# Gated linear attention and SwiGLU on one core: one ordered load queue, part of the transposes by DMA, and new positions for the key, query and output work

## The chip, the cores and the metric

The kernel runs on one core of a Trainium2 chip. A core has a matrix engine (TensorE, PE in the profile, its weight loads apart as PEld), VectorE (DVE), ScalarE (ACT), GpSimd (POOL), and SyncE (SP), which here only issues transfers. All engines run their own queue of instructions in order and wait for one another through semaphores. The metric is device microseconds of one execution; lower is better.

## The reference

For 2048 tokens `x` of width 640, a sigmoid gate mixes two branches: linear attention with a learned softmax feature map (32 heads of 20), and a SwiGLU feed-forward layer of width 1728.

```python
g   = sigmoid((x * gate_w).sum(-1))
q, k, v = split_heads(x @ wqkv)                    # 32 heads of 20
pq, pk  = q @ w_phi[h], k @ w_phi[h]
phi_q = concat(softmax(pq), softmax(-pq));  phi_k likewise
kv  = phi_k^T v ;  z = sum over tokens of phi_k    # per head
o   = (phi_q kv) / (phi_q z + 1e-6)
a   = o @ wo
b   = (silu(x @ w_gate) * (x @ w_up)) @ w_down
out = g * a + (1 - g) * b
```

## The kernel before

Tokens go in 16 tiles of 128; four tiles are a block of 512. All weights stay in SBUF. The whole program is written as work items, each with a position (a number): `put(pos, fn, ...)` collects them, they are sorted, and emitted in that order, so every engine sees its instructions in the order of the positions. `defer(n, fn)` holds a part of an item back until n items (its own among them) are emitted.

The items are:

- `xpose`: transposes a tile of x on PE (5 matmuls with an identity, out of the buffer `xs`), copied by DVE to `xT`. `wxpose`: the same for a 128-row chunk of wk or wq, to `wT`.
- `premult`: multiplies the transposed chunk with the block-diagonal `wbd` of w_phi (built by POOL), so that `wqk` holds wk or wq already times w_phi; its copy out of PSUM is ACT's.
- `vtile` (in short v): x times wv, and in column 641 x times the gate weight (`wvg`), copied by ACT to `v1r` and `svec`.
- `ktile` (k): x times wk-phi, two exponentials on ACT into `ekr`, sums (`ksum`) and reciprocals (`krec`) on DVE, the scaling product on POOL. `kvtile` (kv): 11 matmuls that add phi_k^T v to PSUM banks 6 and 7, over all 16 tiles.
- `kv_finish`, `z_broadcast`: kv and z out of PSUM, z spread over all partitions (`zb`).
- `fitem` (f): one 128-column chunk of gate and up, 10 matmuls of 512 columns, tanh and copy on ACT, one op on DVE (`hT<-hT,ps`, which reads PSUM), one product on POOL. 14 chunks a block; the last is half as long (`wt`).
- `qtile` (q): x times wq-phi, exponentials on ACT into `eq`, then a chain `vec` on DVE (sum `qz`, product `ez` with zb, sum `qw`, five small ops up to `qc`), a product on POOL (`ph`), and a transposing DMA from SP (`phiT`).
- `oitem` (o): 11 matmuls, phi_q times kv, for a block. `ditem` (d): 38 matmuls of 320 columns, the down projection and wo for a tile; ACT scales, SP stores.

PSUM has 8 banks. `next_pair` hands out pairs of banks in a ring, 3 pairs while kv collects in banks 6 and 7, 4 after `widen`. An item must wait until the item that had its pair is read out.

Waits come from a tracker: each operand is an interval of bytes in a partition, and an instruction waits for the writers and readers of all intervals that overlap its own. An operand with strides counts as one interval from its first to its last byte. `wvg[:, :, 0:640]` and its gate column overlap by this rule.

Loads: SP loads tiles of x into six buffers `xs`; tile t+6 is loaded when tile t is transposed. ACT loads wv, wk, wq. POOL loads the gate weight as a column (2-byte elements) and w_phi. The feed-forward weights come at position -0.5 (`load_ffn_weights`, from SP), before the first k.

The first items have positions -10 to -4; k of tile t is at t, kv at t+2.7, v at t-1.2 (from tile 4); f of block 0 from 15.7 on, 0.65 apart; the blocks behind it, from S1 = 24.8 on, have 17.0 each.

Of the kernel before, what the change touches and what calls it, by code (L numbers as in the profile page):

```python
# [14 lines left out]
NCH = 11  # L15
FP = 120 * NCH
# [9 lines left out]
class _Tracker:  # L26
# [32 lines left out]
    def key_of(self, ap):  # L59
        if isinstance(ap, tuple):  # L60
            key = ap
        else:
            space, base = self.base[ap.tensor.name]
            row = 1
            for s in ap.tensor.shape[1:]:
                row *= s
            size = mybir.dt.size(ap.dtype)
            lo = hi = ap.offset % row
            for step, n in list(ap.ap)[1:]:
                if n <= 1:  # L70
                    continue
                if step >= 0:
                    hi += step * (n - 1)
                else:
                    lo += step * (n - 1)
            lo, hi = base + lo * size, base + (hi + 1) * size
# [4 lines left out]
        if key not in self.keyset:  # L81
            self.keyset.add(key)
            self.keys[key[0]].append(key)
            self.lastw[key] = None
            self.readers[key] = {}
        return key
# [18 lines left out]
    def run(self, eng, fn, reads=(), writes=(), dma=False):  # L105
        rkeys = [self.key_of(a) for a in reads]
        wkeys = [self.key_of(a) for a in writes]
# [49 lines left out]
def _build(nc, A_x, A_wqkv, A_w_phi, A_wo, B_x, B_w_gate, B_w_up, B_w_down, gate_w, out):  # L157
# [33 lines left out]
    v1r = sb("v1r", [P, 4, 33 * 21], BF16)  # L191
# [31 lines left out]
    wqn = at("wqn", [P, 5, D], BF16, 14080)  # L223
# [3 lines left out]
    bmask = at("bmask", [P, 5, 8], BF16, 28736)  # L227

# [31 lines left out]
    def transposes(pairs):  # L260
        def fn():
            last = None
            for o, i in pairs:
                last = pe.transpose(o, i, ident[:, :])  # L264
            return last
        return run("pe", fn, [i for _, i in pairs] + [ident[:, :]], [o for o, _ in pairs])
# [53 lines left out]
    def load_x(t):  # L320
        dma("sp", xs[:, t % 6, :], x2[t * P:(t + 1) * P, :])

    load_x(0)
    load_x(1)
    wv_src = A_wqkv[:, 2 * D:3 * D].rearrange("(c p) j -> p c j", p=P)
# [3 lines left out]
    with nc.allow_non_contiguous_dma(reason="gate_w as a column of each chunk"):  # L329
        dma("pool", wvg[:, :, D:D + 1],  # L330
            bass.AP(gate_w.tensor, gate_w.offset, [[1, P], [P, 5], [1, 1]]))
    dma("pool", wph[:, :, :], A_w_phi.rearrange("h e f -> (h e) f").rearrange("(c p) f -> p c f", p=P))
    for t in range(2, 6):
        load_x(t)
    dma("act", wkn[:, :, :], A_wqkv[:, D:2 * D].rearrange("(c p) j -> p c j", p=P))
    dma("act", wqn[:, :, :], A_wqkv[:, 0:D].rearrange("(c p) j -> p c j", p=P))
# [14 lines left out]
    memset("dve", v1r[:, :, :], 0.0)  # L351
# [49 lines left out]
    def xpose(t0, n):  # L401
        pr = next_pair()
        for j in range(n):
            t = t0 + j
            b = 2 * pr + j
            o = bankbf(b, 640)
            transposes([(o[:, c * P:(c + 1) * P], xs[:, t % 6, c * P:(c + 1) * P]) for c in range(5)])
            copy("dve", xT[:, t, :, :].rearrange("p c k -> p (c k)"), o)
            if t + 6 < NT:
                load_x(t + 6)  # L410

    def vtile(t):
        pr = next_pair()
        mm(group(bank(2 * pr, 0, 320), [(xT[:, t, c, :], wvg[:, c, 0:320]) for c in range(5)])
           + group(bank(2 * pr + 1, 0, 321), [(xT[:, t, c, :], wvg[:, c, 320:641]) for c in range(5)]))
        i = halves(pr).rearrange("p b (h d) -> p b h d", d=DH)
        o = v1v[:, t % 4, 0:H, 0:DH].rearrange("p (b h) d -> p b h d", b=2)
        copy("act", o, i)
        copy("act", svec[:, t:t + 1], bank(2 * pr + 1, 320, 321))
# [7 lines left out]
    def tok_proj(t, which):  # L427
        pr = next_pair()
        mm(group(bank(2 * pr, 0, 320), [(xT[:, t, c, :], wqk[:, which, c, 0:320]) for c in range(5)])
           + group(bank(2 * pr + 1, 0, 320), [(xT[:, t, c, :], wqk[:, which, c, 320:640]) for c in range(5)]))  # L430
        return pr

    def ktile(t):
        pr = tok_proj(t, 1)
# [11 lines left out]
    def kvtile(t):  # L446
        b = t % 4
        pairs = []
        for j in range(NCH):
            bk, jj = (KV0, j) if j < 8 else (KV0 + 1, j - 8)  # L450
            o = bank(bk, 63 * jj, 63 * jj + 63, 0, 120)
            pairs.append((o, ekr[:, b, 120 * j:120 * j + 120], v1r[:, b, 63 * j:63 * j + 63],
# [3 lines left out]
    def wxpose(src, m):  # L456
        pr = next_pair()
        o = bankbf(2 * pr, 640)
        transposes([(o[:, c * P:(c + 1) * P], src[:, m, c * P:(c + 1) * P]) for c in range(5)])
# [7 lines left out]
    def premult(which, m):  # L467
        pr = next_pair()
        pairs = []
        for i, (hb, c, c0, c1, off) in enumerate(BANDS):  # L470
            o = bank(2 * pr + hb, c0 - 320 * hb, c1 - 320 * hb)
            pairs.append((o, wT[:, m, c, :], wbd[:, c, off:off + c1 - c0], i in (0, 3), i in (2, 5), True))
        mm(pairs)
        copy("act", wqk[:, which, m, :].rearrange("p (b c) -> p b c", b=2), halves(pr))
# [39 lines left out]
    def qtile(t):  # L514
# [6 lines left out]
        def vec():  # L521
# [201 lines left out]
```

## Time and profile before

| what | value |
|---|---|
| runs | 325.64, 326.25, 327.75 us; median 326.25 us |
| profiled execution, its own time | 327.81 us |
| its span | 326.1 us |
| mean granted PE clock | 0.99 |
| busy share of the span: PE, DVE, ACT, POOL | 92%, 54%, 46%, 47% |
| HBM read and written | 12.56 MB, 2.62 MB |

The span is the time from the first to the last instruction in the profile. A busy PE is the union of matmul records, which overlap their neighbours; what PE needs for an item is read from the start of one item to the start of the next where nothing waits.

### The profile page before, as it was taken

To read this page: it belongs to the slowest core of one execution; us is meant where nothing else is said; L and a number is where in the kernel's file an instruction comes from. 1 tells how busy PE (TensorE), PEld (TensorE's weight loads), DVE (VectorE), ACT (ScalarE), POOL (GpSimd) and SP (SyncE) were. 2 spreads that over 40 slices of the span, in tenths; PEclk is the share of its full clock that TensorE was granted. 3 is DMA by queue.
4 is the path that set the end of the run, shared out by engine and by line. 5 is a ranking of instruction groups with operands and counts; after the bars stand their busy time and mean duration, and the time that the engine had idled before them with its cause. 6 is when DMAs were issued, how large, how long until landed. Compare 5 with 4: busy or idle time off the path is not lost.

```text
span 326.1 us, 4990 instructions
## 1 busy us (share of the span) xinstructions
PE 301.0 (92%) x2041; PEld 182.5 (56%) x2041; DVE 177.5 (54%) x266; ACT 151.4 (46%) x254; POOL 153.4 (47%) x117
## 2 busy tenths in 40 slices
PE   1697899999898986979999999999999999999995
PEld 1364677777444543526555556565554656555773
DVE  6332766675964999892961126697203659721000
ACT  1045466666435654664532643625346363526111
POOL 3500845666784477874372422455624245563000
PEclk9997999999999999979999999999999999999999
DMA  7868962000000033222023000222200022220101
GB/s 261 244 201 278 356 130 77 2 1 2 0 2 1 0 68 66 45 46 64 0 54 78 2 20 0 66 45 64 66 20 0 2 64 46 64 64 2 40 22 40
DMA packets 36077, 21.26 MB, mean 65 GB/s; under 512 B 23816, under 2 KB 36056, under 8 KB 36056
## 3 DMA queue, kind: packets, MB, share of 16 engines
q1 hardware_dynamic: 34024, 18.47, 21.9%
q10 hardware_dynamic: 1968, 2.46, 2.3%
q8 instruction: 16, 0.26, 0.3%
q0 software_dynamic: 64, 0.03, 0.1%
q14 instruction: 5, 0.04, 0.0%
HBM read 12.56 MB, written 2.62 MB: 47 GB/s over the span
## 4 chain that ended last, share of the span: by engine, by line
PE 80%; DVE 9%; ACT 4%; DMA 4%; POOL 1%; issue 1%; POOLq 0%
PE ps L252 79%; DMA wvg<-in_gate_w_dram 2%; DVE qw L291 2%; DVE qz L291 2%; DVE ez L280 2%; DMA wvg<-in_A_wqkv_dram 2%; PE ps L264 2%; POOL ekr L280 1%; DVE hT L284 1%; DVE ksum L291 1%; ACT wqk L270 1%; ACT ekr L270 1%; ACT eq L270 1%; DVE qd L294 0%; ACT v1r L270 0%
## 5 line engine op out<-in xcount | busy, mean ns | idle before, releaser
L280 POOL TENSOR_TENSOR hT<-hT,us 128x512 bf16<-128x512 bf16 (+1 forms) x56 | 68.5, 1235 | 43.6 <-DVE hT L284 43.5
L284 DVE SCALAR_TENSOR_TENSOR hT<-hT,ps 128x512 bf16<-128x512 bf16 (+1 forms) x56 | 37.1, 683 | 63.3 <-ACT hT L270 50.3
L252 PE MATMUL ps<-xT,wg 128*128 128x512 bf16 x260 | 65.7, 384 | 4.0 <-DVE hT L284 3.6
L280 POOL TENSOR_TENSOR ph<-eq,qc 128x1320 bf16<-128x1320 bf16 x16 | 38.8, 2425 | 58.9 <-DVE qc L533 58.9
L252 PE MATMUL ps<-xT,wu 128*128 128x512 bf16 x260 | 64.6, 379 | 0.0
L270 ACT ACTIVATE hT<-ps 128x512 bf16<-128x512 f32 (+2 forms) x60 | 35.8, 596 | 60.0 <-PE ps L252 55.9
L252 PE MATMUL ps<-wd,hT 128*128 128x320 bf16 x448 | 63.5, 299 | 0.0
L252 PEld LDWEIGHTS ps<-wd,hT 128*128 128x128 bf16 x448 | 43.7, 98 | 19.2 <-issue 0.8
L280 POOL TENSOR_TENSOR ekr<-ekr,krec 128x1280 bf16<-128x1280 bf16 x16 | 37.6, 2357 | 34.5 <-DVE krec L294 34.5
L252 PE MATMUL ps<-wqk,xT 128*128 128x320 bf16 x320 | 50.1, 306 | 2.0 <-ACT wqk L270 1.3
L252 PEld LDWEIGHTS ps<-xT,wg 128*128 128x128 bf16 x260 | 25.1, 99 | 32.2 <-DVE hT L284 4.4
L252 PEld LDWEIGHTS ps<-xT,wu 128*128 128x128 bf16 x260 | 25.5, 98 | 31.0 <-issue 0.6
L252 PEld LDWEIGHTS ps<-wqk,xT 128*128 128x128 bf16 x320 | 31.4, 100 | 17.4 <-ACT wqk L270 1.5
L270 ACT ACTIVATE osb<-ps,omg 128x640 bf16<-128x640 f32 x16 | 12.7, 793 | 60.8 <-PE ps L252 60.8
L291 DVE TENSOR_REDUCE ksum<-ekr 128x64 f32<-128x1280 bf16 x16 | 23.7, 1478 | 25.8 <-ACT ekr L270 25.8
L270 ACT ACTIVATE us<-ps 128x512 bf16<-128x512 f32 (+1 forms) x56 | 33.2, 593 | 0.7 <-POOL hT L280 0.6
L291 DVE TENSOR_REDUCE qz<-eq 128x64 f32<-128x1280 bf16 x16 | 23.7, 1482 | 17.4 <-ACT eq L270 17.4
L270 ACT ACTIVATE ekr<-ps 128x640 bf16<-128x640 f32 x32 | 22.5, 703 | 16.6 <-PE ps L252 16.1
L252 PE MATMUL ps<-wvg,xT 128*128 128x320 bf16 (+1 forms) x160 | 25.8, 311 | 2.9 <-DMA wvg<-in_gate_w_dram 2.8
L270 ACT ACTIVATE eq<-ps 128x640 bf16<-128x640 f32 x32 | 22.5, 703 | 5.2 <-PE ps L252 4.7
L252 PE MATMUL ps<-wog,oT 128*128 128x320 bf16 x160 | 24.4, 299 | 0.0
L291 DVE TENSOR_REDUCE qw<-ez 128x64 f32<-128x1280 bf16 x16 | 23.8, 1486 | 0.5
(66 smaller groups left out, 217.1 us busy)
## 6 DMA issues: line engine op xcount, KB each, us to landing
xs<-in_A_x_dram SPq DMA_DIRECT2D x16, 160.0 KB, 5.4
out_dram<-osb SPq DMA_DIRECT2D x16, 160.0 KB, 1.8
wd<-in_B_w_down_dram SPq DMA_DIRECT2D x1, 2080.0 KB, 12.4
wvg<-in_A_wqkv_dram ACTq DMA_DIRECT2D x1, 800.0 KB, 5.3
wkn<-in_A_wqkv_dram ACTq DMA_DIRECT2D x1, 800.0 KB, 9.1
wqn<-in_A_wqkv_dram ACTq DMA_DIRECT2D x1, 800.0 KB, 13.4
wg<-in_B_w_gate_dram SPq DMA_DIRECT2D x1, 800.0 KB, 5.4
wu<-in_B_w_up_dram SPq DMA_DIRECT2D x1, 800.0 KB, 5.8
```

Source lines behind the costliest of these rows:

```text
L252: last = pe.matmul(o, lhsT=l, rhs=r, start=st, stop=sp_, skip_group_check=sk)
L264: last = pe.transpose(o, i, ident[:, :])
L270: return run("act", lambda: act.activation(o, i, func, scale=scale), rd, [o])
L280: return run(e, lambda: eo.tensor_tensor(o, a, b, op), [a, b], [o])
L284: return run("dve", lambda: dve.scalar_tensor_tensor(out=o, in0=a, scalar=s, in1=b, op0=op0, op1=op1), rd, [o])
L291: return run("dve", lambda: dve.tensor_reduce(o, i, AX.X, ALU.add), [i], [o])
```

## The change

- **Loads.** All big loads go through SP's queue in one written order: x0, half of wv, x1, the other half of wv, x2, x3, wk, x4, x5, and then, by transposing DMA straight from HBM, x6 into `xT`, wq into `wTq`, and x7 to x15 into `xT`. So 10 of 16 tiles of x and all of wq are no longer transposed on PE, nor copied by DVE. Each item `xpose` now has one tile. The feed-forward weights keep their place behind the last load of x.
- **Gate weight.** It is loaded by ACT as 5 rows of 128 (`gwr`), transposed on PE in one matmul (`gcol`), and copied by DVE into the column of `wvg`. w_phi is loaded by ACT too.
- **Start.** Six memsets go from DVE to POOL, behind `wbd`; the one of `v1r` shrinks to its last head. v is split in halves (`vhalf`), so that its first half needs half of wv. Six tiles of v (before: four) come ahead of the first k. The copy out of `premult` for wk alternates between DVE and ACT. The ring has 4 pairs up to position 3.5.
- **Tracker.** A strided operand in SBUF of up to 16 pieces is now tracked piece by piece (`keys_of`).
- **k and q** run chunk by chunk, the two halves inside; the first k is split into five parts with waits of their own.
- **Positions.** kv at t+3.6 (before t+2.7), v at t-2.2 (before t-1.2) with 6 buffers (before 4); kv_finish, z_broadcast somewhat later; q, o and d re-spaced; the DVE chain of q in two parts, with one item's work between them: `vec_a` is `qz` and `ez`, `vec_b` the rest.

SP's queue at the start. `wg`, `wu`, `wd`, `wog` are the feed-forward and output weights. Before:

```order
L306 DMA xs<-in_A_x_dram 128x640 x12
L306 DMA wg<-in_B_w_gate_dram 128x5x512
L306 DMA wu<-in_B_w_up_dram 128x5x512
L306 DMA wg<-in_B_w_gate_dram 128x5x640
L306 DMA wu<-in_B_w_up_dram 128x5x640
```

SP's queue at the start in the change:

```order
L321 DMA xs<-in_A_x_dram 128x640
L321 DMA wvg<-in_A_wqkv_dram 128x5x320
L321 DMA xs<-in_A_x_dram 128x640
L321 DMA wvg<-in_A_wqkv_dram 128x5x320
L321 DMA xs<-in_A_x_dram 128x640 x2
L321 DMA wkn<-in_A_wqkv_dram 128x5x640
L321 DMA xs<-in_A_x_dram 128x640 x2
L320 DMA_TRANSPOSE xT<-in_A_x_dram 128x5x128
L320 DMA_TRANSPOSE wTq<-in_A_wqkv_dram 128x5x128 x5
L320 DMA_TRANSPOSE xT<-in_A_x_dram 128x5x128 x9
L321 DMA wg<-in_B_w_gate_dram 128x5x512
```

The parts of wqkv now stand between the tiles of x, and 15 transposing loads stand between them and the feed-forward weights.

PE at the first k (`ps<-wqk,xT`, 10 matmuls each) up to the next v. `ps<-ident,...` are transposes, `ps<-wbd,...` is premult. Before:

```order
L252 MATMUL ps<-wqk,xT 128x320 x20
L264 MATMUL ps<-ident,wqn 128x128 x5
L264 MATMUL ps<-ident,xs 128x128 x10
L252 MATMUL ps<-wqk,xT 128x320 x10
L252 MATMUL ps<-v1r,ekr 120x63 x11
L252 MATMUL ps<-wvg,xT 128x320 x5
```

PE at the same place in the change (premult of wq is now `ps<-wbd,wTq`, of which one stands in full here):

```order
L267 MATMUL ps<-wvg,xT 128x321 x5
L267 MATMUL ps<-wqk,xT 128x320 x30
L267 MATMUL ps<-wbd,wTq 128x140 x2
L267 MATMUL ps<-wbd,wTq 128x80 x2
L267 MATMUL ps<-wbd,wTq 128x140 x2
L267 MATMUL ps<-wqk,xT 128x320 x10
```

Three k in a row, a premult of wq and a fourth k stand where two k, three transposes and a third k stood; three more premults and the first kv (`ps<-v1r,ekr`) follow, so that the first kv comes behind four k instead of three, and behind four of the five premults of wq.

DVE around the second and third q in the change (`hT<-hT,ps` is the op of an f; the chain of q runs from `qz` to `qc`); before, `qz` to `qc` stand without a break and two or three `hT<-hT,ps` between one chain and the next:

```order
L306 TENSOR_REDUCE qz<-eq 128x64
L295 TENSOR_TENSOR ez<-eq,zb 128x1280
L299 SCALAR_TENSOR_TENSOR hT<-hT,ps 128x512
L306 TENSOR_REDUCE qw<-ez 128x64
L299 SCALAR_TENSOR_TENSOR qw<-qz,qw 128x64
L568 TENSOR_TENSOR qm<-qw,qz 128x64
L295 TENSOR_TENSOR qd<-qm 128x32
L309 RECIPROCAL qd<-qd 128x32
L573 SCALAR_TENSOR_TENSOR qc<-qz,g,qd 128x64
L299 SCALAR_TENSOR_TENSOR hT<-hT,ps 64x512
```

One `hT<-hT,ps` now stands inside the chain.

The diff, cut to its core:

```diff
+NPE = 6
+NV = 6
...
-    def key_of(self, ap):
+    def keys_of(self, ap):
...
+        if space == "sbuf" and dims:
+            lo, hi = extent(off, dims[1:])
+            step, n = dims[0]
+            if step > hi - lo + 1 and n <= 16:
+                parts = [(lo + step * i, hi + step * i) for i in range(n)]
...
-    wqn = at("wqn", [P, 5, D], BF16, 14080)
+    wTq = at("wTq", [P, 5, 5, P], BF16, 14080)
+    gwr = at("gwr", [P, P], BF16, 28864)
...
     def load_x(t):
-        dma("sp", xs[:, t % 6, :], x2[t * P:(t + 1) * P, :])
+        if t < NPE:
+            dma("sp", xs[:, t, :], x2[t * P:(t + 1) * P, :])
+        else:
+            dma("sp", xT[:, t, :, :], x2[t * P:(t + 1) * P, :], transpose=True)
...
+    dma("act", gwr[0:5, :], bass.AP(gate_w.tensor, gate_w.offset, [[P, 5], [1, P]]))
+    dma("act", wph[:, :, :], ...)
     load_x(0)
+    dma("sp", wvg[:, :, 0:320], wv_src[:, :, 0:320])
     load_x(1)
-    dma("act", wvg[:, :, 0:D], wv_src)
+    dma("sp", wvg[:, :, 320:D], wv_src[:, :, 320:D])
+    load_x(2)
+    load_x(3)
+    dma("sp", wkn[:, :, :], wk_src)
+    for t in range(4, 7):
+        load_x(t)
+    for m in range(5):
+        dma("sp", wTq[:, m, :, :], A_wqkv[m * P:(m + 1) * P, 0:D], transpose=True)
+    for t in range(7, NT):
+        load_x(t)
...
-        dma("pool", wvg[:, :, D:D + 1],
-            bass.AP(gate_w.tensor, gate_w.offset, [[1, P], [P, 5], [1, 1]]))
-    dma("pool", wph[:, :, :], ...)
-    dma("act", wkn[:, :, :], ...)
-    dma("act", wqn[:, :, :], ...)
...
-    memset("dve", v1r[:, :, :], 0.0)
+    memset("dve", v1v[:, :, H, :], 0.0)
...
-    memset("dve", ones[:, :], 1.0)
-    memset("dve", kvsb[:, :, :], 0.0)
-    memset("dve", eq[:, :, 1280:FP], 0.0)
-    memset("dve", qc[:, :, :], 0.0)
-    memset("dve", ph[:, :, :], 0.0)
-    memset("dve", wog[:, :, :], 0.0)
+    memset("pool", wog[:, :, :], 0.0)
+    memset("pool", ones[:, :], 1.0)
+    memset("pool", kvsb[:, :, :], 0.0)
+    memset("pool", eq[:, :, 1280:FP], 0.0)
+    memset("pool", qc[:, :, :], 0.0)
+    memset("pool", ph[:, :, :], 0.0)
...
+    def gcol():
+        pr = next_pair()
+        o = bankbf(2 * pr, 8)[:, 0:5]
+        transposes([(o, gwr[0:5, :])], 5)
+        copy("dve", wvg[:, :, D:D + 1], o.unsqueeze(2))
...
+    def tok_proj(t, which, split=False):
+        pr = next_pair()
+        pairs = [(bank(2 * pr + hb, 0, 320), xT[:, t, c, :], wqk[:, which, c, 320 * hb:320 * hb + 320],
+                  c == 0, c == 4, False) for c in range(5) for hb in range(2)]
...
-        copy("act", wqk[:, which, m, :]..., halves(pr))
+        copy("dve" if which and m % 2 == 0 else "act", wqk[:, which, m, :]..., halves(pr))
...
-        defer(1, vec)
+        defer(1, vec_a)
+        defer(2, vec_b)
...
+    ring["n"] = 4
+    put(-20, xpose, 0)
+    put(-20, gcol)
+    put(-19, vhalf, 0, 0)
+    put(-18.5, xpose, 1)
+    put(-18, vhalf, 0, 1)
...
+        put(-13 + 0.1 * m, wxpose, m)
+        put(-10 + 0.1 * m, premult, 1, m)
+        put((2.1, 3.1, 3.3, 3.4, 4.4)[m], premult, 0, m)
...
+    put(3.5, ring3)
+    put(-7, load_ffn_weights)
...
-        put(t + 2.7, kvtile, t)
+        put(t + 3.6, kvtile, t)
...
-        put(NT + 3.65 + 1.6 * u, qtile, u)
+        put(NT + 4.4 + 2.7 * t if t < 4 else S1 + 6.2 + 3.4 * (t - 4), qtile, t)
...
-                put(a + SL * (0.22 + 0.12 * u), qtile, 4 * s + u)
+        o0, d0, dd = {1: (10.8, 12, 1.5), 2: (5.2, 7, 3.1), 3: (1.7, 4, 4.4), 4: (-1.3, 2, 4)}[s]
...
```

More of the change, by code (lines that the diff above doesn't have):

```diff
@@ L80, in key_of @@
             key = (space, lo, hi)
[L81 to L86, printed above, removed]
+            if key not in self.keyset:
+                self.keyset.add(key)
+                self.keys[space].append(key)
+                self.lastw[key] = None
+                self.readers[key] = {}
+            out.append(key)
+        return out
     def _conflicts(self, key):
@@ L258, in group, with transposes @@
         return [(o, l, r, i == 0, i == n - 1, False) for i, (l, r) in enumerate(lr)]
-    def transposes(pairs):
+    def transposes(pairs, k=P):
         def fn():
@@ L263, in fn @@
             for o, i in pairs:
-                last = pe.transpose(o, i, ident[:, :])
+                last = pe.transpose(o, i, ident[0:k, 0:k])
             return last
@@ L471, in premult @@
             o = bank(2 * pr + hb, c0 - 320 * hb, c1 - 320 * hb)
-            pairs.append((o, wT[:, m, c, :], wbd[:, c, off:off + c1 - c0], i in (0, 3), i in (2, 5), True))
+            pairs.append((o, (wT if which else wTq)[:, m, c, :], wbd[:, c, off:off + c1 - c0], i in (0, 3), i in (2, 5), True))
         mm(pairs)
-        copy("act", wqk[:, which, m, :].rearrange("p (b c) -> p b c", b=2), halves(pr))
+        copy("dve" if which and m % 2 == 0 else "act", wqk[:, which, m, :].rearrange("p (b c) -> p b c", b=2), halves(pr))
     def kv_finish():
```

139 lines of the change are left out of this document (70 added, 69 removed).

## The prediction

> **What bounds the kernel now.** I read the page first: how busy each engine is, and at which clock.
>
> ```profile
> span 326.1 us, 4990 instructions
> PE 301.0 (92%) x2041; PEld 182.5 (56%) x2041; DVE 177.5 (54%) x266; ACT 151.4 (46%) x254; POOL 153.4 (47%) x117
> PEclk9997999999999999979999999999999999999999
> ```
>
> PE is the bound on average, but 92% hides where the other 25 us are. The chain that ended last shows the places; its columns are start, length, and what ran.
>
> ```profile
> 6.36 6.17 DMA wvg<-in_gate_w_dram
> ...
> 12.67 4.38 PE ps L252 x20
> ...
> 26.19 2.86 PE ps L252 x10
> ...
> 45.88 0.28 PE ps L264 x5
> ...
> 141.71 180.94 PE ps L252 x1103
> ...
> 322.67 0.79 ACT osb L270
> ```
>
> PE's real work starts at 12.67 us, when the column of gate weights lands; the first k starts at 26.19 us. From 141.71 us on PE runs to 322.65 us without a gap, and 3.45 us of copy and store follow. So only what lies ahead of 141.71 us can be taken away. What PE waited for (total, times, longest):
>
> ```profile
> PE ps L264 <- DMA xs<-in_A_x_dram: 7.0, 4, 3.4
> PE ps L252 <- DVE hT L284: 6.4, 4, 2.5
> PE ps L252 <- DMA wvg<-in_gate_w_dram: 2.8, 1, 2.8
> PE ps L252 <- POOL ekr L280: 2.3, 2, 1.5
> PE ps L252 <- ACT wqk L270: 1.3, 1, 1.3
> PE ps L252 <- ACT zb L270: 0.4, 1, 0.4
> ```
>
> Loads cost 9.8 us, all at the start; DVE's op of an f costs 6.4 us, in the stage with q at 98 to 142 us. The rest of the start is seen in a table by stage (span, busy us per engine, clock, DMA share, GB/s):
>
> ```profile
> 3.40:12.64 9.24, 2.86 (x20) 1.80 (x20) 6.25 (x14) 0.33 (x1) 3.77 (x13) 1.00 1.07 353
> 26.19:29.05 2.86, 2.86 (x11) 1.64 (x12) 0.00 (x0) 0.00 (x0) 0.00 (x0) 0.50 1.05 348
> 118.36:125.63 7.27, 4.77 (x26) 2.37 (x26) 7.06 (x11) 3.68 (x7) 5.23 (x4) 1.00 0.27 52
> ```
>
> The first k runs at a clock of 0.50. In the q stage DVE is full (7.06 of 7.27 us) while PE is not.
>
> **What PE needs, item by item.** Where nothing waits, an item costs the distance between starts. PE in order of time:
>
> ```profile
> 76.86 0.74 PE L252 MATMUL ps<-v1r,ekr 128*120 128x63 bf16 x11
> 77.44 1.53 PE L252 MATMUL ps<-wvg,xT 128*128 128x320 bf16 x10
> 78.81 1.52 PE L252 MATMUL ps<-wqk,xT 128*128 128x320 bf16 x10
> ...
> 133.47 1.24 PE L252 MATMUL ps<-xT,wg 128*128 128x512 bf16 x5
> ...
> 135.63 1.24 PE L252 MATMUL ps<-xT,wg 128*128 128x512 bf16 x5
> ...
> 146.52 3.97 PE L252 MATMUL ps<-wd,hT 128*128 128x320 bf16 x28
> ...
> 151.69 1.52 PE L252 MATMUL ps<-wqk,xT 128*128 128x320 bf16 x10
> ```
>
> kv 0.58 us; v 1.37, and k and q, of the same shape, too; f 2.16 (its half-long chunk 1.08); d 5.17. That is 0.43 ns a column (1.37 us for 3200), so o (5632 columns) takes 2.4, premult (720) 0.31, z_broadcast (1320) 0.6; five transposes take 0.28 (the chain's row at 45.88).
>
> A test: behind 141.71 us stand 34 f with 3 half chunks, 16 d, 10 q and 3.6 o: 73.4 + 3.2 + 82.7 + 13.7 + 8.7 = 181.7 us, against 180.94 measured. Sums by these rows are 0.4% high.
>
> **The change, part by part.** From the start of the first k on, PE does 16 k and 16 q (43.8), 10 v (13.7), 16 kv (9.3), 52 f and 4 half chunks (116.6), 4 o (9.6), 16 d (82.7), five premults (1.6), z_broadcast (0.6): 277.9, less 0.4% **276.8 us**. The 15 groups of transposes that stood here (4.2 us by 0.28 each) are gone, and two v moved ahead of the first k.
>
> *The start.* DMA moves 353 GB/s from 3.40 to 12.64 us. At that rate, in the written order, 1.15 MB (x0, x1 and all of wv) are in at about 6 us, wk (2.3 MB) at about 9.5, x5 at about 10.5. I add 0.5 us for wv's rows of 640 bytes. The first x was there at 3.44 us, and its five cold transposes took 0.71 us:
>
> ```profile
> 3.44 0.71 PE L264 MATMUL ps<-ident,xs 128*128 128x128 bf16 x5 [3.44 <-DMA xs<-in_A_x_dram]
> ```
>
> The copies behind a transpose and behind a premult (busy us, mean ns):
>
> ```profile
> L276 DVE COPY xT<-ps 128x640 bf16<-128x640 bf16 x16 | 6.8, 469 | 6.5 <-PE ps L264 6.5
> L270 ACT ACTIVATE wqk<-ps 128x640 bf16<-128x640 f32 x10 | 6.6, 718 | 0.0
> ```
>
> The gate weight no longer holds v back: 5 rows come with the first x and cost one short matmul and a copy. I walk on: first half of v at 5 us, cold, twice its warm time (1.4); x1's transposes; second half at 7 to 8.4; x2, x3 to 9.4; v1 to v3 warm, to 13.5; x4 and five chunks of wk to 15.2 (1.7 of PE; DVE's copies, 0.47 each, run on to 17.1); x5 and v4 to 17.2; five premults to 18.9, their copies (0.72) now on two engines; v5 to 20.3. w_phi's 640 rows of 40 bytes run beside x0 and wv; I take 0.7 us, bounds 0 and 3 (the 2.6 us that the first x took). The first k starts at **21.0 us** (19.5 to 24), after two more v than before.
>
> A rule weighed here: "TensorE: Matmul & The Clock Gate", Part 1, in the Trainium skill, says that an idle window of about 3.4 us halves the clock, and a busy one restores it. The row at 26.19 us agrees (0.50, ten matmuls in 2.86 instead of 1.37), after a stretch in which PE was half idle. By the rule the longest waits of the walk are too short for it and nothing is added; were the clock lost again, the first k's would take some 1.5 us more.
>
> *The first kv.* Four k follow at once, and the engines behind them set the pace:
>
> ```profile
> L270 ACT ACTIVATE ekr<-ps 128x640 bf16<-128x640 f32 x32 | 22.5, 703 | 16.6 <-PE ps L252 16.1
> L291 DVE TENSOR_REDUCE ksum<-ekr 128x64 f32<-128x1280 bf16 x16 | 23.7, 1478 | 25.8 <-ACT ekr L270 25.8
> L294 DVE RECIPROCAL krec<-ksum 128x64 f32<-128x64 f32 x16 | 8.9, 553 | 0.6
> L280 POOL TENSOR_TENSOR ekr<-ekr,krec 128x1280 bf16<-128x1280 bf16 x16 | 37.6, 2357 | 34.5 <-DVE krec L294 34.5
> ```
>
> ACT needs 1.44 us a k and 0.72 a premult. Four k and the third premult of wq are read out 8.1 us after the first k ends; v6 takes the pair of banks of that premult. PE has 5.9 us of work until then: **2.2 us** lost (bounds 0 and 3.5, the ekr and wqk waits of before). The first kv itself is ready 6.3 us after that k (0.2 + 1.44 + 1.48 + 0.55 + 2.36 and hand-overs), ahead of its turn at 6.7. POOL has room for the six memsets moved to it: it waited up to 16.2 us for its first ekr, and none of them took DVE longer than 1.8 us, so at most 11 us at DVE's speed; without that room they would cost what reaches past the first kv.
>
> ```profile
> POOL ekr L280 <- DVE krec L294: 34.5, 14, 16.2
> L298 DVE MEMSET ph<- 128x2112 uint32 x1 | 1.8, 1818 | 0.4 <-issue 0.4
> ```
>
> After this, PE has 3.3 us a tile and POOL 2.36, so it stays dense.
>
> *z_broadcast* keeps two f behind the last kv and its wait: **1.3 us** (0.9 of DVE's wait and the 0.4 on zb).
>
> *The q stage.* DVE's chain of one q and two f, from chain row to chain row:
>
> ```profile
> 111.63 1.40 DVE qz L291
> ...
> 117.71 1.19 DVE hT L284 x2
> 118.90 1.40 DVE qz L291
> ```
>
> 7.27 us, 6.1 of them the q; PE needs 2 x 2.16 + 1.37 = 5.7. In the change q0 and q1 have four f between them (PE 10.0, DVE 8.6): dense. But q1 to q5 have 2.5, 2, 2 and 3: PE 6.8, 5.7, 5.7, 7.9; DVE 8.0, 7.3, 7.3, 8.0. DVE falls 4.5 us behind before the first d gives it 17 us for one q. The ring of four pairs absorbs a part; walking the two queues, PE waits 0.9, 1.3 and 1.7: **3.9 us** (bounds 0 and 5.5, before's waits there, 6.4 less 0.9). From q6 on there are at least 10 us of PE for 8 of DVE, dense as before.
>
> *Transposing loads.* The nearest row is phiT, 11 squares of 128 instead of 5:
>
> ```profile
> L305 SPq DMA_TRANSPOSE phiT<-ph x16: 1372/1389/1532, 113.0 to 287.4; - x16
> DMA to landing us min/median/max: 3.5/3.5/3.7
> 163.00:165.00 2.00, 2.00 (x17) 1.42 (x16) 1.97 (x2) 0.00 (x0) 2.00 (x2) 1.00 0.75 142
> ```
>
> SP issues one in 1.39 us: 15 take at most 21, done by about 25 us, and behind them wait only the feed-forward weights, wanted at about 80. A load from HBM is not shown before. Its bounds: phiT's bytes at the DMA share of that window, about 1.6 us for 11 squares or 0.75 for 5 (15 loads in 11 us, none late); and 3.5 us each without overlap. Then wq's fourth chunk and x7 on come late by up to 4 us in sum, since k takes a tile every 3.3 us. I take the near end, **0**.
>
> Sum: 21.0 + 276.8 + 2.2 + 1.3 + 3.9 + 3.45 = **308.7 us** of span, 17.4 less than 326.1. The profiled execution took 327.81 us, 1.7 around its span, so 310.4 by its measure; the runs' median is 326.25, and 17.4 less is **309 us**.
>
> **Rivals.**
>
> *A: loads in single file.* Each waits for the one before, at phiT's 3.5 us. 309 + 4 = 313. For it: one queue. Against it: the plain loads in that queue overlap (353 GB/s).
>
> *B: DVE owns the q stage,* and the walk at the start is too kind: all of 5.5, and 24 us to the first k: 309 + 1.6 + 3 = 314. For it: DVE 7.06 of 7.27.
>
> *C, slower than before: a transposing load has a price by the square.* v15 is reached at about 61 us (13 k, 10 kv, 9 v, five premults behind 21.0 + 2.2). With 15 loads in file from 11 us (x5 and the added 0.5), x15 lands at 11 + 15p. All of the gain is gone at 61 + 17 = 78 us, so from p = 4.5 us on. At 6 us a load x15 lands at 101: 309 + 40 = 349. Against it: phiT moved 11 squares in 3.5 us. "VectorE: DVE Perf Modes", The three transpose paths, in the Trainium skill, gives 1309 ns for a 128 x 128 transpose by DMA; were that paid by each of five squares in turn, an estimate from that page is 6.5 us a load and 357 us. phiT's 3.5 us, where the same reckoning gives 14.4, speaks against it.
>
> *D: the re-spacing brings DVE nothing to wait for, and the start goes by the plain walk:* 309 - 3.9 - 0.7 = 304.
>
> **How the numbers follow.** Forecast (305 to 312) 0.65, A 0.12, B 0.10, C 0.05, D 0.08. The range 303.5 to 316.5 takes in all but C and what two bounds at once would add. 1% (3 us) is about what a measurement of this kernel tells from no change. Faster by over 1%: all but C and a few unseen waits, 0.93; within 1%: 0.03; slower: 0.04.
>
> **What the profile after would show.** Right: first k at 20 to 22 us and a clock of 1.00 there; no wait of PE for xT or wTq; a wait on wqk or ekr of about 2 us before v6; DVE's hT waits of about 4 to 5 us in all; PE without gaps from about 130 us on. A wait of PE on a DMA behind 25 us speaks for A or C. Wrong would make it above all a price of the transposing loads that phiT doesn't show, or a start held up by SP's single queue.

## The result, and the profile after

| | before | change |
|---|---|---|
| runs | 325.64, 326.25, 327.75, 327.76 us | 306.99, 308.59, 310.29, 309.89 us |
| median | 327.0 us | 309.24 us |
| profiled execution, span | 326.1 us | 305.3 us |
| granted clock in it | 0.99 | 1.00 |

The ratio is 0.9452 (95% interval 0.9384 to 0.9519): 5.5% faster. The forecast was 309.0 us.

The page of the change, the same three rows as before:

```profile
span 305.3 us, 4854 instructions
PE 291.9 (96%) x1967; PEld 178.2 (58%) x1967; DVE 163.7 (54%) x249; ACT 149.4 (49%) x251; POOL 156.5 (51%) x121
PEclk9999999999999999999999999999999999999999
```

PE is busy 9 us less, and idle 13.4 us instead of 25.1. The clock's row has no dip left, where before had one at the first k and one at 140 to 160 us.

The start, in PE's timeline of the change (start, length, operands, and in brackets the wait ahead of it):

```profile
5.41 1.49 PE L267 MATMUL ps<-wvg,xT 128*128 128x320 bf16 x5 [1.40 <-DMA wvg<-in_A_wqkv_dram]
...
20.73 4.24 PE L267 MATMUL ps<-wqk,xT 128*128 128x320 bf16 x30
...
28.48 0.76 PE L267 MATMUL ps<-v1r,ekr 128*120 128x63 bf16 x11 [0.83 <-ACT ekr L285]
29.70 1.52 PE L267 MATMUL ps<-wvg,xT 128*128 128x320 bf16 x10 [0.46 <-ACT wqk L285]
```

The first v starts at 5.41 us instead of 12.67, the first k at 20.73 instead of 26.19, behind six v instead of four, and it runs at full clock: three k in 4.24 us. The q stage, and the z_broadcast ahead of it, in the same view:

```profile
84.74 0.33 PE L267 MATMUL ps<-dz,ones 120*128 120x360 bf16 x1 [0.40 <-DVE hT L299]
...
127.46 1.66 PE L267 MATMUL ps<-phiT,kvsb 120*64 120x512 bf16 x11 [0.78 <-DVE hT L299]
131.76 1.25 PE L267 MATMUL ps<-xT,wg 128*128 128x512 bf16 x5 [2.65 <-DVE hT L299]
```

All that PE waited for in the change (total, times, longest):

```profile
PE ps L267 <- DVE hT L299: 4.3, 4, 2.6
PE ps L279 <- DMA xs<-in_A_x_dram: 3.2, 1, 3.2
PE ps L267 <- DMA wvg<-in_A_wqkv_dram: 1.4, 1, 1.4
PE ps L267 <- ACT ekr L285: 0.8, 1, 0.8
PE ps L267 <- ACT wqk L285: 0.5, 1, 0.5
```

No row names a load behind wv: PE never waited for a tile of x or a chunk of wq that came by transposing DMA. The wait on the gate weight's column is gone, and POOL's on `ekr` too. What is left is 4.6 us for the first loads, 1.3 at the first kv, and 4.3 on DVE's op of an f.

Where the 20.8 us between the two profiled spans went, by places: the first k starts 5.5 earlier; behind it, PE has two v less (2.7) and 15 groups of transposes less (4.2); the first k lost 1.5 to the clock before and nothing now; the waits on `hT` and `zb` fell from 6.8 to 4.3 (2.5); before lost 1.6 right behind 141.71 us (its clock from 140 to 160 us was 0.91); the waits between the first k and the next v fell from 2.2 to 1.3 (0.9); a second wait of before on POOL's `ekr`, 0.8 at 83.10 us, is gone; the tail is 0.5 shorter. That is 20.2. The other 0.6 us are short gaps and aren't split up here.

**The spread of the runs.** Each run has its granted clock beside its span. Of the change: 305.3 us at 1.000, 306.9 at 0.993, 308.6 and 308.2 at 0.989; another four runs gave 305.3 at 1.000 and 306.7 to 307.0 at 0.994. Of before: 324.1 to 324.7 at 1.000, 325.9 to 326.3 at 0.99. So the same program has two or three times, and the clock sorts nearly all of them (one run of before has 324.1 at 0.995, and of the tracker alone, experiment 8, 322.4 and 322.5 at 0.995 stand beside 322.6 at 1.000). At full clock on both sides the change is 324.3 to 305.3, **19.0 us**. Below, "at full clock" means spans of runs at 0.999 or 1.000, against 305.3.

### The profile page after: what moved, and what is told of

Same layout as the page of the kernel before. It is cut to its first block, busy times and chain, and to the rows that moved or that the text cites. A ratio compares the mean times of both kernels' runs of the same rounds, so it can differ in the third digit from the quotient of the medians.

```text
span 305.3 us, 4854 instructions
## 1 busy us (share of the span) xinstructions
PE 291.9 (96%) x1967; PEld 178.2 (58%) x1967; DVE 163.7 (54%) x249; ACT 149.4 (49%) x251; POOL 156.5 (51%) x121
## 3 DMA queue, kind: packets, MB, share of 16 engines
HBM read 10.10 MB, written 2.62 MB: 42 GB/s over the span
## 4 chain that ended last, share of the span: by engine, by line
PE 77%; DVE 16%; ACT 4%; DMA 1%; issue 1%; SPq 0%
PE ps L267 76%; DVE hT L299 3%; DVE qz L306 3%; DVE qw L306 3%; DVE ez L295 3%; ACT ekr L285 2%; ACT eq L285 1%; DMA wvg<-in_A_wqkv_dram 1%; PE ps L279 1%; DVE dz L295 1%; DVE qd L309 1%; ACT wqk L285 1%; DVE qc L573 1%; DVE qw L299 0%; DVE qm L568 0%
## 5 line engine op out<-in xcount | busy, mean ns | idle before, releaser
L295 POOL TENSOR_TENSOR hT<-hT,us 128x512 bf16<-128x512 bf16 (+1 forms) x56 | 66.4, 1195 | 60.1 <-DVE hT L299 60.1
L267 PE MATMUL ps<-xT,wg 128*128 128x512 bf16 x260 | 64.6, 379 | 3.1 <-DVE hT L299 3.1
L267 PE MATMUL ps<-wqk,xT 128*128 128x320 bf16 x320 | 48.4, 299 | 0.0
```

What stands on the lines that cost most here:

```text
L267: last = pe.matmul(o, lhsT=l, rhs=r, start=st, stop=sp_, skip_group_check=sk)
L295: return run(e, lambda: eo.tensor_tensor(o, a, b, op), [a, b], [o])
```

## The experiments

Each kernel ran beside runs of before on the same chip. All are the changed kernel with the edit shown, except the tracker alone, which is the kernel before.

**1. The change unedited, again.** No edit. The question was whether the clock accounts for the spread of its runs.

> The changed kernel once more, unedited, so that the others are compared with it on the same chip. Its runs so far had spans of 305.3, 306.9, 308.2 and 308.6 us at mean granted PE clocks of 1.000, 0.993, 0.989 and 0.989. Theory K: the spread is the clock alone, lost once or twice after a stall of PE: span = 305.3 + 306 x (1 - clock), within 0.5 us, in every run. Rival: the spread is elsewhere (loads, DMA), and span and clock go apart by 1 us or more.

Measured: median 308.47 us (307.04 to 308.74), ratio 0.9425 (0.9388 to 0.9462). One run at full clock, 305.3 us, and three at 0.994 with 306.7, 306.8 and 307.0. Theory K's formula gives 307.1 at 0.994 and is off by 0.1 to 0.4 there. Spans in between without a drop of the clock don't occur.

**2. The old spacing of q, o and d.**

```diff
-        defer(2, vec_b)
+        defer(1, vec_b)
-        put(NT + 4.4 + 2.7 * t if t < 4 else S1 + 6.2 + 3.4 * (t - 4), qtile, t)
+        put(NT + 4.4 + 1.6 * t if t < 4 else S1 + SL * (t // 4 - 1) + SL * (0.22 + 0.12 * (t % 4)), qtile, t)
-        o0, d0, dd = {1: (10.8, 12, 1.5), 2: (5.2, 7, 3.1), 3: (1.7, 4, 4.4), 4: (-1.3, 2, 4)}[s]
...
```

> The change with its re-spacing of q, o and d undone (the positions of before, moved by 0.75 for the four q of block 0, and the DVE chain of q whole); loads, transposes and start stay. Theory P (the prediction): the q stage is bound by DVE either way; its waits for hT go from 3.4 to about 5.5 us, so the kernel gets about 2 us slower than the change (311). Rival R: the spacing carries the larger part of the gain; 8 us or more slower (317 or more).

Measured: median 308.69 us (308.37 to 308.99), ratio 0.944 (0.9409 to 0.9472). At full clock 306.5 and 306.7: the re-spacing is worth 1.3 us. PE's timeline of this kernel at the q stage shows what is behind it, and more:

```profile
109.88 1.25 PE L267 MATMUL ps<-xT,wg 128*128 128x512 bf16 x5 [0.83 <-DVE hT L299]
...
116.11 1.25 PE L267 MATMUL ps<-xT,wg 128*128 128x512 bf16 x5 [2.54 <-DVE hT L299]
117.20 2.19 PE L267 MATMUL ps<-xT,wu 128*128 128x512 bf16 x5
119.19 2.03 PE L267 MATMUL ps<-xT,wg 128*128 128x512 bf16 x5
...
128.17 3.96 PE L267 MATMUL ps<-wd,hT 128*128 128x320 bf16 x28 [0.65 <-issue]
```

DVE's waits sit in the same stage as in the change (3.9 us from 100 to 140 us, against 3.4), with another 0.65 of issue: the waits grew by 0.5, not by the 2.1 that theory P had, and the time by 1.3 instead of 2. Rival R is refuted. And 1 us behind the wait of 2.54 the same five matmuls take 2.19 and 2.03 instead of 1.24: in this run the stall also cost the clock.

**3. q1 to q6 put further apart.** The waits at 127 and 132 us were read as DVE falling behind between q1 and q5. Here the items of q are spaced so that three f (two and a half between q1 and q2) stand between one q and the next, ahead of the first d.

```diff
-        put(NT + 4.4 + 2.7 * t if t < 4 else S1 + 6.2 + 3.4 * (t - 4), qtile, t)
+        put((20.4, 22.3, 24.2, 27.9, 31.5, 37.0, 38.6)[t] if t < 7 else S1 + 6.2 + 3.4 * (t - 4), qtile, t)
```

> The change with other positions for the second to seventh q: three f (not 2, 2 and 3) between one q and the next in the stage before the first d, and the sixth and seventh q behind the first and second d. Theory P: DVE then keeps up (8.05 us of DVE for 7.9 of PE a q); PE's waits for hT there fall from 3.4 us to under 1, and the span at full clock from 305.3 to about 302.5. Theory K adds: with this stall gone the clock is lost less often, so the runs spread less. Rival: the stall moves (to the o items, whose phiT comes later) and nothing is won.

Measured: median **304.66 us** (304.42 to 304.87), ratio 0.9317 (0.9287 to 0.9347). The only wait left in the stage, in PE's timeline of this kernel:

```profile
127.46 0.62 PE L267 MATMUL ps<-phiT,kvsb 120*64 120x512 bf16 x3 [1.04 <-DVE hT L299]
```

The waits there fell from 3.43 to 1.04 us, by 2.4, and the span at full clock fell from 305.3 to 302.9, by 2.4. The median fell by more, 3.8 us: all four runs were at full clock, 302.7 to 303.1. So the stall in the q stage is what made the change's runs fall apart, and its price is its own length plus, in most runs, 1.4 to 3.3 us of clock.

**4. All transposes back on PE, with a shared buffer.** x6 to x15 and wq loaded plainly and transposed on PE again; the plain copy of wq was put into memory that `ekr` uses later.

```diff
-            dma("sp", xT[:, t, :, :], x2[t * P:(t + 1) * P, :], transpose=True)
+            dma("sp", xs2[:, t - NPE, :], x2[t * P:(t + 1) * P, :])
-        dma("sp", wTq[:, m, :, :], A_wqkv[m * P:(m + 1) * P, 0:D], transpose=True)
+    dma("sp", wqn[:, :, :], A_wqkv[:, 0:D].rearrange("(c p) j -> p c j", p=P))
+        put((1.05, 1.1, 2.05, 2.06, 3.05)[m], wxpose, m, wqn, wTq)
+            put(t - t % 2 - 4.05, xpose, t)
```

> The change with x6 to x15 and wq loaded plainly and transposed on PE, with copies by DVE, as before; the order of the queue and all other positions stay. Theory P: PE is dense there, so its 15 groups of five transposes add 15 x 0.28 = 4.2 us (313.5), and ring and DVE up to 1 us more. Rival H: the transposes lay in PE's gaps, and the loads are what costs: within 1.5 us of the change.

Measured: median 334.3 us (333.67 to 334.69), ratio 1.0223 (1.0181 to 1.0265). This says nothing about the transposes. DVE's timeline of this kernel shows why:

```profile
14.10 0.12 DVE L317 MEMSET ekr<- 128x80 uint32 x1 [12.04 <-DMA wqn<-in_A_wqkv_dram]
14.20 0.17 DVE L317 MEMSET krec<- 128x132 f32 x1
14.29 0.43 DVE L295 COPY xT<-ps 128x640 bf16<-128x640 bf16 x1
```

A memset of 0.12 us waited 12.04 us for the load that now shared its bytes; behind it in DVE's queue stood the copy of the first tile, and PE's first v came at 14.77 us instead of 5.41.

**5. The same, with no memory shared with `ekr`.** The plain wq takes the place of `wTq`.

```diff
-    wTq = at("wTq", [P, 5, 5, P], BF16, 14080)
+    wqn = at("wqn", [P, 5, D], BF16, 14080)
+        put((1.05, 1.1, 2.05, 2.06, 3.05)[m], wxpose, m, wqn)
+            put(t - t % 2 - 4.05, xpose, t)
...
```

> x6 to x15 and wq again loaded plainly and transposed on PE with copies by DVE, in the queue order and at the positions of the change; the plain wq now lies where the change has its transposed wq, so that no buffer is shared with ekr. Theory P: 15 groups of five transposes cost PE 15 x 0.28 = 4.2 us; at the first k, DVE's copies of wq stand behind sums that wait for ACT, which costs up to 3 us more. Span at full clock 309.5 to 312.5, against 305.3. Rival H: the transposes lay in PE's gaps; 305 to 307.

Measured: median 322.48 us (319.56 to 324.43), ratio 0.9839 (0.9774 to 0.9903). At full clock 317.5 us (one run): 12.2 more than the change, where 4.2 to 7.2 was expected. From PE's timeline of this kernel (its profiled run had a clock of 0.984):

```profile
21.53 2.88 PE L269 MATMUL ps<-wqk,xT 128*128 128x320 bf16 x20
...
28.97 2.85 PE L269 MATMUL ps<-wqk,xT 128*128 128x320 bf16 x10 [2.50 <-DVE wT L293]
...
38.87 1.54 PE L269 MATMUL ps<-wvg,xT 128*128 128x320 bf16 x10 [0.60 <-DVE wT L293]
```

v6 starts at 38.87 us instead of 29.70. The third k waits 2.50 us for the copy of a transposed chunk of wq, and then runs cold: ten matmuls in 2.85 instead of 1.52. This run took 322.3 us, and it lost another 2.6 to the clock behind the wait in the q stage, so the trace shows places, not the parts of the 12.2. The expected size fell; the next two runs take the two halves apart, with some of the transposes at other positions.

**6. Only x6 to x15 on PE.**

```diff
-            dma("sp", xT[:, t, :, :], x2[t * P:(t + 1) * P, :], transpose=True)
+            dma("sp", xs2[:, t - NPE, :], x2[t * P:(t + 1) * P, :])
+            put(-9.56 if t < 8 else t - t % 2 - 4.05, xpose, t)
```

> Only x6 to x15 on PE (plain loads, transposes with copies by DVE; x6 and x7 ahead of the first k, the others two by two as before); wq stays with the transposing DMA. Theory P': a group of transposes costs its 0.28 us of PE, and more only where its copy waits in DVE's queue behind sums that wait for ACT, which was the wq part of the run before. So 10 x 0.28 = 2.8 us, and under 1.5 more: span at full clock 308.1 to 309.6, against 305.3. Rival: the copies of x in DVE's queue hold v back in the whole k stage; 311 or more.

Measured: median 315.97 us (312.42 to 317.05), ratio 0.9636 (0.957 to 0.9701); at full clock (one run) 310.7, 5.4 more than the change, where 2.8 to 4.3 was expected. The ten groups alone are 2.8. From PE's timeline of this kernel:

```profile
21.67 4.24 PE L269 MATMUL ps<-wqk,xT 128*128 128x320 bf16 x30
...
30.55 0.87 PE L269 MATMUL ps<-v1r,ekr 128*120 128x63 bf16 x11 [1.96 <-ACT wqk L287]
31.24 2.86 PE L269 MATMUL ps<-wvg,xT 128*128 128x320 bf16 x10
```

The first k is 0.9 later, with two of the groups ahead of it; the first kv waits 1.96 us, where the two waits of the change there were 1.3; and in this run v6 behind it runs cold (2.86 instead of 1.52). Three short waits on `svec`, which the change doesn't have, add 0.9.

**7. Only wq on PE,** all five chunks ahead of the first k.

```diff
-        dma("sp", wTq[:, m, :, :], A_wqkv[m * P:(m + 1) * P, 0:D], transpose=True)
+    dma("sp", wqn[:, :, :], A_wqkv[:, 0:D].rearrange("(c p) j -> p c j", p=P))
+        put(-9.58, wxpose, m, wqn)
```

> Only wq on PE (plain load), and its five transposes and copies ahead of the first k, where DVE has room; x6 to x15 stay with the transposing DMA. Theory P': 5 x 0.28 = 1.4 us, none of the waits for wT that the run with both showed; span at full clock 306.7 to 307.5. Rival: wq on PE costs as much wherever it stands, 309 or more.

Measured: median 314.36 us (313.7 to 315.32), ratio 0.9599 (0.9558 to 0.964). No run was at full clock; the best was 311.5 at 0.995. By the change's own slope (3.1 us for 0.011) the four runs give estimates of 308.4 to 310.1, or 3.1 to 4.8 more than the change, where at most 2.2 was expected. PE's timeline of this kernel:

```profile
19.05 1.99 PE L279 MATMUL ps<-ident,wqn 128*128 128x128 bf16 x25
...
22.35 4.24 PE L267 MATMUL ps<-wqk,xT 128*128 128x320 bf16 x30
...
31.83 0.79 PE L267 MATMUL ps<-v1r,ekr 128*120 128x63 bf16 x11 [2.62 <-ACT wqk L285]
32.46 2.33 PE L267 MATMUL ps<-wvg,xT 128*128 128x320 bf16 x10
```

The transposes push the first k by 1.6 us, near the 1.4 expected. What was not expected is the first kv: a wait of 2.62 us for `wqk`, with cold matmuls behind it in the profiled run; all four runs are below full clock. The reason is the ring. Five groups take five turns in it, so each item behind them meets another pair. The first kv writes banks 6 and 7, which up to position 3.5 are the ring's fourth pair, so it waits until that pair's last user is read out. Counted from the positions, that user is the fourth k in the change, the third premult of wq in experiment 6, and the fourth premult here. ACT's timeline of this kernel has that copy as the last of these three:

```profile
29.89 1.89 ACT L285 ACTIVATE wqk<-ps 128x640 bf16<-128x640 f32 x3
```

They end at 31.78 us, and the kv starts at 31.83. Its own operand was not late: POOL's first product on `ekr` starts at 27.61 us and takes 2.36. By the same shift the f behind z_broadcast gets the pair of z_broadcast's first part and waits 0.9 us for `zb`, as in experiment 9. The profiled run lost some 1.7 us to the clock behind the first kv and 2.4 behind the wait in the q stage, which the change has too; without them it would be at an estimated 309.1. The 3.8 more than the change are what the places give: 1.6 at the first k, 1.3 more at the first kv, 0.9 at `zb`. No run moved the ring alone.

**8. The tracker alone.** The kernel before, with only `keys_of` of the change.

```diff
-    def key_of(self, ap):
+    def keys_of(self, ap):
...
+        if space == "sbuf" and dims:
+            lo, hi = extent(off, dims[1:])
+            step, n = dims[0]
+            if step > hi - lo + 1 and n <= 16:
+                parts = [(lo + step * i, hi + step * i) for i in range(n)]
```

> The kernel before with one part of the change alone: the tracker that follows strided operands piece by piece. Its gate column is then no longer taken to overlap wv, and POOL issues that load at once. Theory P: the column's 6.2 us from issue to landing ran behind a wait of 4.8 us that only the tracker made; v starts at about 9.8 us (DVE's memsets end at 9.3) instead of 12.67, and the time falls by 2 to 3 us (325 at the lower clock of before). Rival: wk is what comes last at the start; v starts earlier and then waits, and the time stays within 1 us.

Measured: median 325.38 us (324.17 to 326.44), ratio 0.996 (0.9936 to 0.9985). At full clock 322.6, against 324.1 to 324.7: 1.7 us, a little less than expected. The first v no longer waits for the gate weight's column, but PE's waits of this kernel name the next thing that is late:

```profile
PE ps L276 <- DMA xs<-in_A_x_dram: 8.5, 4, 3.5
```

7.0 us before, 8.5 now: v starts at 11.17 us instead of 12.67, since the fourth tile of x is only transposed at 10.66. With the loads in three queues the tiles of x come in no better order, and the tracker's freedom is worth 1.7 of the 19 us. The rest of the start's gain comes with the other edits. The one load queue is the likely carrier, but it was not run alone, and no run splits this part.

**9. wk by transposing DMA too.** Five more of these loads, ahead of the other 15.

```diff
-    dma("sp", wkn[:, :, :], wk_src)
+        dma("sp", wT[:, m, :, :], A_wqkv[m * P:(m + 1) * P, D:2 * D], transpose=True)
-        put(-13 + 0.1 * m, wxpose, m)
...
```

> The change with wk too loaded by transposing DMA (five more such loads, ahead of that of x6 and behind x5), its 25 transposes and five copies gone. Theory P: loads overlap and SP issues one in 1.3 us, so the last chunk is in at about 15 us, before PE wants it at about 17; the first k starts 1.5 us earlier (19.2 instead of 20.7), span at full clock about 303.8. Rival A (a price by the load): chunks land one after the other at 3.7 us each, the last at about 23; PE waits for wT and the first k starts at 25 or later, span 309 or more.

Measured: median 308.67 us (306.88 to 309.85), ratio 0.9441 (0.9393 to 0.9489); at full clock 305.1, or 0.2 less than the change. SP's queue and PE in the timelines of this kernel:

```profile
4.76 7.17 SPq L320 DMA_TRANSPOSE wT<-in_A_wqkv_dram  x5
```

```profile
15.41 1.53 PE L267 MATMUL ps<-wvg,xT 128*128 128x320 bf16 x10 [0.31 <-DVE xT L291]
...
19.95 4.24 PE L267 MATMUL ps<-wqk,xT 128*128 128x320 bf16 x30
...
28.24 0.79 PE L267 MATMUL ps<-v1r,ekr 128*120 128x63 bf16 x11 [1.36 <-ACT wqk L285]
...
85.14 1.25 PE L267 MATMUL ps<-xT,wg 128*128 128x512 bf16 x5 [0.90 <-ACT zb L285]
```

Five loads, all issued by 11.9 us, were not waited for by premult at 16.8. Rival A is refuted. The first k comes 0.8 us earlier, instead of 1.5, and PE is still 0.83 ahead at the last matmul of z_broadcast (83.91 us against 84.74 in the change). The f behind it then waits 0.90 for `zb`, and the gain is gone. That wait is the ring's too: five groups of transposes less shift the pairs, and this f gets the one that z_broadcast's first part had. Counted so for the other kernels, experiments 7 and 10 have the same pair and wait 0.9, experiment 5 has the second part's and waits 1.3, and in the change, and in experiments 3, 6 and 11, this f has a free pair and no wait for `zb` shows.

**10. Both of 3 and 9.** The edits of 3 and 9 together.

> Both edits at once: the other positions of q (e3) and wk by transposing DMA (e6). They lie in different stages, so theory P adds them: span at full clock about 302.9 - 1.5 = 301.4, time about 303.1. Rival: what the start wins, the q stage or the first kv gives back; 302.9 as with the positions alone.

Measured: median 304.54 us (304.17 to 305.05), ratio 0.9324 (0.9282 to 0.9366); spans 302.4 to 303.3, against 302.7 to 303.1 of experiment 3. It adds nothing, where 301.4 was expected: the wait on `zb` is there again (0.9). The twelve runs of experiments 3, 10 and 11 all have a clock of 0.999 or more; of the twelve runs with the change's positions of q (the change, its repeat and experiment 9), nine don't.

**11. A warm PE at the start.** Experiment 3, with 14 and 9 matmuls of 128 columns on the identity ahead of the first v, whose results nobody reads.

```diff
+    def warmup(n):
+        mm([(bank(7, 0, 128), ident[:, :], ident[:, :], True, True, False) for _ in range(n)])
+    put(-20.5, warmup, 14)
+    put(-19.5, warmup, 9)
```

> The change with the other positions of q (e3), and 14 matmuls of 128 columns on the identity ahead of the first transposes and 9 behind the gate row's, into a bank that nothing reads: work that the kernel doesn't need, while PE would wait for loads. Theory C (clock): until 9.9 us PE runs at half speed (five matmuls of 320 columns in 1.49 us instead of 0.7); begun earlier, full speed comes earlier, and the first k starts 1 to 2 us sooner (about 19.3): span about 301.4, against 302.9. Rival: loads set the pace up to 9.9 us, and the span stays within 0.4 us.

Measured: median **303.8 us** (303.52 to 304.0), ratio 0.9282 (0.9249 to 0.9315), the fastest version. From PE's timeline of this kernel:

```profile
5.38 0.84 PE L267 MATMUL ps<-wvg,xT 128*128 128x320 bf16 x5 [0.39 <-DMA wvg<-in_A_wqkv_dram]
...
7.58 0.84 PE L267 MATMUL ps<-wvg,xT 128*128 128x321 bf16 x5 [1.08 <-DMA wvg<-in_A_wqkv_dram]
...
20.07 2.20 PE L267 MATMUL ps<-wqk,xT 128*128 128x320 bf16 x15
```

The first half of v takes 0.84 us instead of 1.49 (the granted clock does not show this: in the change it reads 1.00 from 5.4 to 9.9 us), but then the second half of wv is late by 1.08. About half of the expected gain comes out: the first k 0.66 earlier, spans of 301.8 to 302.3 against 302.9.

## Why the prediction was right, point by point

**The first k** was put at 21.0 us and came at 20.73. The walk holds stage by stage, each stage 0.2 to 0.8 us later than forecast: first half of v forecast at 5 us, seen at 5.41; v5's end at 20.3, seen at 20.73. The loads came at about the rate read from before (366 GB/s from 5.4 to 9.9 us, against 353). The term that failed here is w_phi's: its many small rows, priced at 0.7 us with a bound of 3, held nothing up. POOL had them at 5.87 us, and the premults start at 17.64. That the 0.7 made up for the walk's 0.4 is luck.

**The transposing loads** were put at 0, the near end, and no wait of PE names them. SP's part in the timeline and in the view of the tiles (duration min/median/max in ns), and their time to landing, in the change:

```profile
5.52 1.29 SPq L320 DMA_TRANSPOSE xT<-in_A_x_dram  x1
6.86 7.85 SPq L320 DMA_TRANSPOSE wTq<-in_A_wqkv_dram  x5
14.75 12.36 SPq L320 DMA_TRANSPOSE xT<-in_A_x_dram  x9
27.16 0.59 SPq L321 DMA_DIRECT2D wg<-in_B_w_gate_dram  x1
```

```profile
L320 SPq DMA_TRANSPOSE xT<-in_A_x_dram x10: 1277/1278/1802, 5.5 to 25.8; - x10
DMA to landing us min/median/max: 3.0/3.7/6.1
```

One is issued about every 1.4 us while each takes 3.7 to land: they overlap. Rival A (single file) is refuted here, and again by experiment 9 with 20 of them. Rival C needed 4.5 us a load one behind the other, so that x15 lands at 78 us; the 15 were issued in 21.6 us, the last at 25.8, and none took over 6.1 to land. "VectorE: DVE Perf Modes", The three transpose paths, in the Trainium skill, gives 1309 ns for a 128 x 128 transpose by DMA; paid for each of five squares in turn, an estimate from that page is 6.5 us a load. The trace has 3.7 to landing, for five squares, and 1.4 between loads, so that figure is not a price that adds up over squares.

**The first kv** was put at 2.2 us lost and cost 1.3, by the two resources named, `ekr` and `wqk`, at the place named, ahead of v6. The wait on `ekr` is not for the kv's operand: it ends with ACT's exponentials of the fourth k, which has banks 6 and 7 (experiment 7). POOL's memsets cost nothing on the path, as said, though they took longer than on DVE.

**z_broadcast** was put at 1.3 and cost 0.40: the wait on `zb` is gone from the list, not only DVE's shorter. The prediction had no reason for that; the f behind z_broadcast happens to get a pair that is free (experiment 9).

**The q stage** was put at 3.9 us and cost 3.43, in two waits where the walk of the two queues had three (0.9, 1.3, 1.7). Experiment 3 shows the mechanism: three f to each q, and 2.4 of it are gone. Rival B (all of 5.5) and rival D (nothing) both fail on this number.

**The dense PE work** was 276.8 us from the first k on. Measured: 302.33 - 20.73 = 281.6, less the waits behind it (0.83, 0.46, 4.32) is 276.0. Inside it, **o was mis-sized**: priced by its columns at 2.4 us for 11 matmuls, where the row at 127.46 us shows 11 in 1.66, with the tail of the last one, and the other o take about 1.55. Four o cost some 3.4 us less: 277.9 - 3.4 = 274.5, and 1.5 us of short gaps stand beside that. The test of the prices on before (181.7 against 180.94) had hidden it: the 3.6 o there were 3.1 us too dear, but that stretch had lost 1.6 us to the clock in its first 18 us, and the rest of the difference lay in short gaps.

**The sum and the clock.** The forecast's span was 308.7 us, and the profiled execution has 305.3: 3.4 too much, made of 0.3 at the first k, 0.8 in the dense work, 0.9 each at the first kv and at zb, 0.5 at q and 0.5 at the tail, less one wait of 0.49 on `hT` at 231.61 us that was not foreseen. What brought the median back onto 309 is luck, and something that the sum had no term for: three of the four runs lost 1.6 to 3.3 us to the clock. The sum put nothing for the clock at the start, which held in the profiled run, and did not ask what the q stage's stall does to it. The -17.4 has the same flaw on its other side, since it starts from an execution of before at 0.99; at full clock on both sides the difference is 19.0.

**What the transposes on PE were worth** was counted as 4.2 us of PE. Putting them back into the changed order costs more (experiments 5 to 7): 5.4 us for the tiles of x, an estimated 3.1 to 4.8 for wq, 12.2 for both. Each group is 0.28 us of PE, but it also takes a turn in the ring of pairs, and so changes whom the first kv waits for: that wait grows from 1.3 to 2 or 2.6 us, and in the profiled runs the matmuls behind it run cold. It takes a copy in DVE's queue too, for which k waited 2.50 us in experiment 5. The rest of the 12.2 is not taken apart by any run. The sum in the prediction came out because it counted the waits of the new order by themselves.

## What to carry to other kernels

Price an item that is taken off the critical engine with the buffers and the queue turns that it also held, not by its busy time alone; undoing it shows the difference. Where buffers go round in a ring, count who had the buffer before: a few turns more or less decided here what the first kv and the f behind z_broadcast waited for, and once took back a whole gain of 0.8 us. When runs of one kernel fall into two or three times, set each beside its granted clock before comparing medians, and look for the stall that lets the clock go: here cutting a stall from 3.4 to 1.0 us gained 3.8 in the median, and made the runs agree within 0.5 us. A row that prices an item by its columns holds for the shape it was read from.

## What the runs showed of the hardware that was not expected

**Short stalls cost the clock, in some runs.** PE's timeline of the kernel before, right behind the stage with q:

```profile
141.71 1.67 PE L252 MATMUL ps<-phiT,kvsb 120*64 120x512 bf16 x7 [1.85 <-DVE hT L284]
143.31 2.30 PE L252 MATMUL ps<-xT,wg 128*128 128x512 bf16 x5
```

Five matmuls in 2.30 us instead of 1.24, after a wait of 1.85; in experiment 2 after one of 2.54, in experiment 7 after 2.62. In the change's profiled run a wait of 2.65 cost nothing, while six of its eight runs show a clock of 0.989 to 0.994. Experiment 9 leaves the q stage as in the change, and PE's timeline of its profiled run (0.994) has the same wait with a loss behind it:

```profile
132.00 1.53 PE L267 MATMUL ps<-xT,wg 128*128 128x512 bf16 x5 [2.65 <-DVE hT L299]
133.32 2.34 PE L267 MATMUL ps<-xT,wu 128*128 128x512 bf16 x5
```

From there to the first matmul on `wog` it takes 7.66 us at a granted clock of 0.78, the change 5.98 at 1.00. "TensorE: Matmul & The Clock Gate", Part 1, in the Trainium skill, puts the loss behind an idle window of about 3.4 us, and says that the window runs freely. Waits shorter than that were enough here. That the same wait costs in one run and not in the next would fit a window that doesn't start with the wait; but a wait of 1.85 us doesn't fill a window of 3.4 wherever that starts, so the rule as it stands doesn't account for these losses, and no run here shows what does.

**A transposing load takes SP nearly as long for 5 squares as for 11:** 1.28 us against 1.39 for phiT. The 15 loads of 5 squares filled SP's queue for 21.6 us.

**A memset's time goes by its elements, on POOL as on DVE.** In POOL's timeline of the change

```profile
7.91 2.76 POOL L313 MEMSET wog<- 128x3200 bf16 x1
...
11.67 3.62 POOL L313 MEMSET ph<- 128x4224 bf16 x1
```

against 1.39 and 1.82 us on DVE for the same bytes, there as half as many elements of 4 bytes. It is the elements, and not the engine, that doubled the time: DVE's timeline of the kernel before has one with elements of 2 bytes,

```profile
1.46 2.37 DVE L298 MEMSET v1r<- 128x2772 bf16 x1 [1.46 <-PEq L708]
```

which is 0.85 ns an element, as on POOL (0.86), and as for DVE's elements of 4 bytes (0.87 and 0.86). The six memsets moved at no cost only because POOL waited for its first `ekr` anyway.
